# Attention and a gated two-layer network on one core: the largest of v spread by TensorE, stores issued by ScalarE from spare weight rows, five softmax buffers

## The chip, the cores and the metric

The kernel runs on one core of a Trainium2 chip. The metric is the device time of one execution in microseconds. The core has five engines that run their own instruction queues in order and meet at semaphores: TensorE (PE in the profile, with its weight loads as PEld), VectorE (DVE), ScalarE (ACT), GpSimd (POOL) and SyncE (SP), which here only issues DMAs.

## The reference, cut to what matters

Eight batches of eight heads, 576 queries and keys, 64 columns a head. Scores below the row's largest minus tau are dropped before the softmax. The result, 4608 tokens of 512 columns, goes through a network with 2048 hidden columns.

```python
scores = scale * np.matmul(q, k.transpose(0, 1, 3, 2))
thresh = np.max(scores, axis=-1, keepdims=True) - tau
scores = np.where(scores >= thresh, scores, -1000000000.0)
scores = scores - np.max(scores, axis=-1, keepdims=True)
attn = np.exp(scores)
attn = attn / (np.sum(attn, axis=-1, keepdims=True) + 1e-09)
x = np.matmul(attn, v)            # then heads side by side
h = x @ w_in
out = (h * (1.0 / (1.0 + np.exp(-h)))) @ w_out
```

Inputs of q, k, v are float32; the weights come as float64 and are decoded on the core.

## The kernel before

**Precision by halves.** Most products run on a high and a low half (hi + lo) of each factor: float16 for x, v, the attention weights, g and the layers' weights; the products hi·hi, hi·lo and lo·hi are summed in PSUM. To use float16's range, v and the weights are scaled by a power of two that comes from their largest magnitude.

**The scale of v.** For each batch, `vmax` (line 233) takes the largest magnitude of each of four loads of v per partition. `vscale` (line 243) calls `pow2_scales`, which reduces the four to one number per partition (`v_one`, line 110), spreads the largest over all partitions with GpSimd's `partition_all_reduce` (`v_all`, line 113), and works out the scale and its inverse with small VectorE instructions (`v_cl`, `v_e`, `v_sc`, lines 116 to 132). The scale is used where ScalarE and VectorE split v (lines 270 and 271) and in the factors of the network. The scales of the weights (`across=False`) don't go through line 113.

**Tiles of attention.** A tile is 128 queries of one head; there are 288, 36 in a batch. For a tile TensorE makes the scores in PSUM (line 406; line 394 for the first sixteen, which work in float32 throughout), VectorE their negative maximum (416) and threshold (419), ScalarE the exponential into a buffer `w32` (426), VectorE the mask and the sum (435) and the reciprocal (439, 443), ScalarE the division in place (448). GpSimd rounds the weights to float16 (459) and takes the low half (462 and 465) into `hl`; then `w32` is free again. SyncE issues DMA transposes of `hl` into `wT` (475), from which TensorE makes the product with v (490). There are four `w32` buffers and three of `hl`.

**Units of the network.** An h unit is twelve matmuls (524) into a PSUM bank, then tanh on ScalarE (532), a product on VectorE (533), the high half of g on ScalarE (541) and the low half on VectorE (547). An o unit is twelve matmuls (562) over a quarter of g; four quarters fill one bank, and after the fourth ScalarE copies it to a tile `o` of 128 x 288 (571) in one of two buffers and SyncE stores it (573): 64 stores in all. Both kinds and some others take their banks in turn from `bank` (two at first, three later).

**The order.** The loop at line 695 goes over tiles and calls the steps in slots; `todo` gives loads and splits of v, q and k their slots (a batch that starts at tile u has its `vscale` at u - 2, its first split of v at u + 4, its first product with v at u + 11), and `credit` spreads units among the tiles. The framework then orders each engine's queue by a simulated timeline and priorities, so steps can move ahead of their slots where their data and buffers allow. SyncE's one queue holds all loads, transposes and stores.

**The weights' tile.** `wst` (line 138) has 32 + 2 rows of 512 columns: raw weights are decoded two rows ahead of the split ones that take their place, so once all are split the last two rows hold nothing that is read again.

Of the kernel before, what the change touches and what calls it, by code (L numbers as in the profile page):

```python
# [10 lines left out]
BF16 = mybir.dt.bfloat16  # L11
# [8 lines left out]
P = 128  # L20
# [6 lines left out]
WID = 320  # L27
EXPMASK = 0x7F800000
GB = 17  # buffers of g: a group of 16 and one ahead
WSPARE = 2  # raw weights lie this far ahead of the split ones, which take their place  # L30
LOAD = 5  # tiles that the loads of q and k run ahead
AV_LAG = 3  # tiles from a visit's last to its product with v
EARLY = 36  # tiles in which ACT still rounds the weights of attention for GpSimd
GAP, GAP1 = 12, 1  # free slots before batch 0's second visits and before batch 1
V_SLOT = 26  # batch 0's values are split from here on
RATES = (1.3, 0.8)  # units of the experts per slot while batch 0's two groups are there
RATE = 0.95
# weights: first chunk, slots of the decoding and of the splitting, priority
W_PLAN = ((0, 0, 10, 13, 0), (16, 9, 22, 26, 150))
PRI_S, PRI_SOFT1, PRI_SOFT2 = 500, 50, 200  # L40

# a visit of two heads: its tiles of 128 queries (4: the last 64 of both heads) for the
# first and the second head, and the query ranges that it completes
VISITS = {
# [7 lines left out]
def attention_moe(  # L52
# [20 lines left out]

    # three banks in turn; the last one is for the sums of the weights while they come in
    turn = [0, 2]
# [5 lines left out]

    # ---------------------------------------------------------------- constants
    tau_sb = const.tile([P, 1], F32, name="tau_sb")
    nc.sync.dma_start(out=tau_sb, in_=tau)
    # 1/8 where the threshold can be met (tau >= 0), else 0: all scores equal, all kept
    gate = const.tile([P, 1], F32, name="gate")
# [7 lines left out]

    # stacks of (hi; lo) rows of q, with 64 zero columns for the shared tile
    qstack = []
# [8 lines left out]
    def pow2_scales(mx, name, across=True):  # L105
        """From mx [P, n] (bounds >= 0, per partition or, without across, the same on all):
        s = 2^(13-e) and 1/s for the largest's exponent e."""
        k = name[0]
        one = const.tile([P, 1], F32, name=f"{name}_one", tag=f"{k}_one")
        nc.vector.tensor_reduce(out=one, in_=mx, op=ALU.max, axis=AX.X)  # L110
        if across:
            allp = const.tile([P, 1], F32, name=f"{name}_all", tag=f"{k}_all")
            nc.gpsimd.partition_all_reduce(allp, one, P, bass.bass_isa.ReduceOp.max)
            one = allp
        cl = const.tile([P, 1], F32, name=f"{name}_cl", tag=f"{k}_cl")
        nc.vector.tensor_scalar(
            out=cl, in0=one, scalar1=2.0**-20, scalar2=2.0**47, op0=ALU.max, op1=ALU.min
        )
        e2 = const.tile([P, 2], I32, name=f"{name}_e2", tag=f"{k}_e2")
        nc.vector.tensor_scalar(  # L120
            out=e2[:, 0:1], in0=cl.bitcast(I32), scalar1=EXPMASK, scalar2=None, op0=ALU.bitwise_and
        )
        nc.vector.tensor_scalar(
            out=e2[:, 1:2], in0=cl.bitcast(I32), scalar1=EXPMASK, scalar2=EXPMASK,
            op0=ALU.bitwise_and, op1=ALU.bitwise_xor,
        )
        sc = const.tile([P, 2], F32, name=f"{name}_sc", tag=f"{k}_sc", bufs=3)
        nc.vector.tensor_scalar(
            out=sc[:, 0:1], in0=e2[:, 1:2].bitcast(F32), scalar1=2.0**12, scalar2=None, op0=ALU.mult
        )  # L130
        nc.vector.tensor_scalar(
            out=sc[:, 1:2], in0=e2[:, 0:1].bitcast(F32), scalar1=2.0**-13, scalar2=None, op0=ALU.mult
        )
        return sc

    # ---------------------------------------------------------------- weights
    NW = NK * 4 + NF
# [28 lines left out]
    def decode_weights(i):  # L166
        """float64 words to float32: the sign, 8 bits of the exponent (2^-112 on the top word
        read as float32 takes the exponent's bias down), 23 of the fraction."""
        t = wraw.pop(i)
# [13 lines left out]
        )  # L183
        # sums of the magnitudes over the rows of four chunks, four columns at a time: they
        # bound h (w_in), w_out
        n, c = divmod(i, 4)
# [31 lines left out]

    # ---------------------------------------------------------------- values
    vmx = {}  # L220
# [54 lines left out]

    # ---------------------------------------------------------------- q and k
    qkraw = {}
# [11 lines left out]
    def qcol(h, i):  # L289
        """Column of query tile i in the stack (even: 0..3, last, zeros; odd: zeros, last,  # L290
        2, 3, 0, 1)."""
        return i * P if h % 2 == 0 else (0, 384, 512, 128, 256)[(i + 1) % 5]
# [29 lines left out]

    # the first visits work in float32 throughout: the tensor engine has time for them
    direct = {}
# [51 lines left out]

    # ---------------------------------------------------------------- scores
    # a tile: (visit, [(head, query tile, first row, rows)])
    sps = {}
# [31 lines left out]
    def soft1(t):  # L411
        s_ps = sps[t]
        sm = sb.tile([P, 5], F32, tag="small", name=f"sm_{t}", bufs=4)
        w = sb.tile([P, S], F32, tag="w32", name=f"w32_{t}", bufs=4)
        negm, thr = sm[:, 0:1], sm[:, 1:2]
        nc.vector.tensor_reduce(  # L416
            out=negm, in_=s_ps[:, :, :HALF], op=ALU.max, axis=AX.XY, negate=True
        )
        nc.vector.tensor_scalar(
            out=thr, in0=negm, scalar1=-1.0, scalar2=ntau, op0=ALU.mult, op1=ALU.add  # L420
        )
        small[t] = sm
        wtile[t] = w
# [52 lines left out]

    # ---------------------------------------------------------------- attn @ v
    x16 = {}

    def av(v, p, c0, n):  # L480
        """w @ v of the pair's two heads, side by side in the columns of the array: (w hi + w lo) @
        v hi + w hi @ v lo."""
        b = visits[v][0]
# [29 lines left out]

    # ---------------------------------------------------------------- experts
    gt = {}
# [39 lines left out]
    def o_unit(b, c0, n, d, quarter):  # L555
# [11 lines left out]
        def post():  # L567
            if quarter < 3:
                return
            o = sb.tile([P, WID], F32, tag="o", name=f"ot_{b}_{c0}_{d}", bufs=2)  # L570
            nc.scalar.activation(o[:, :n], ps[:, :n], AF.Copy, scale=moe_sc[b][:, 1:2])
            c = b * S + c0
            nc.sync.dma_start(out=outT[d * P : (d + 1) * P, c : c + n], in_=o[:, :n])

# [8 lines left out]

    # ---------------------------------------------------------------- schedule
    visits = [(0, p, kind) for kind in ("low", "high") for p in range(NPAIR)]
# [195 lines left out]
```

## Time and profile before

| | us |
|---|---|
| median of three timed runs (lowest, highest) | 1358.73 (1357.87, 1359.26) |
| span of the profiled execution | 1360.4 |
| TensorE matmuls busy | 1183.7 (87%) |
| VectorE busy | 1002.8 (74%) |
| ScalarE busy | 817.5 (60%) |
| GpSimd busy | 789.9 (58%) |

The profile is one execution. "Busy" leaves out register, semaphore and DMA-issuing instructions. A slice line gives the busy share in tenths in 40 equal parts of the span. A line of waits reads: who waited, for whom, us in total, times, longest. A group's line reads: line, engine, operation, output and input, count, then busy us and mean ns of one, then idle time just before. A window's line gives start and end, length, busy us of PE, PEld, DVE, ACT and POOL (with counts), the TensorE clock that was granted as a share of full speed, the DMA share and GB/s. "Issue" as the end of an idle time means that nothing the profile shows was waited for.

### The profile page before, as it was taken

How to read it: one execution, taken by the hardware profiler on the slowest of the kernel's cores; microseconds unless marked ns; L12 is line 12 of the kernel's file. 1: busy time of each engine (PE TensorE's matmuls, PEld its weight loads, DVE VectorE, ACT ScalarE, POOL GpSimd, SP SyncE). 2: the span in 40 equal slices, each digit the busy share in tenths (PEclk: the TensorE clock that was granted, in tenths of full speed). 3: DMA queues.
4: the chain of work that ended last, by engine and by line, in shares of the span. 5: the costliest groups of instructions: out<-in, count | busy, mean ns of one | idle time of the engine just before them, and what ended most of it. 6: DMA issues, size and time to landing. Idle time of an engine off the chain costs nothing.

```text
span 1360.4 us, 26858 instructions
## 1 busy us (share of the span) xinstructions
PE 1183.7 (87%) x9392; PEld 899.9 (66%) x9392; DVE 1002.8 (74%) x2619; ACT 817.5 (60%) x1493; POOL 789.9 (58%) x964
## 2 busy tenths in 40 slices
PE   3774787898599979898899969899799999999998
PEld 2453555666477757676677757677577777777777
DVE  4987997897598967968497856869478787872421
ACT  3776775675476756656375745757367666662432
POOL 2647984787478656754476646556467666661000
PEclk9887888999799999999899979999799999999999
DMA  6454955778467656664475556565466565543000
GB/s 226 140 185 125 197 129 94 146 139 170 88 133 155 122 106 129 131 128 86 99 132 124 118 96 136 101 127 121 82 122 116 115 129 115 106 88 53 6 19 18
DMA packets 363479, 158.15 MB, mean 116 GB/s; under 512 B 329552, under 2 KB 338256, under 8 KB 363344
## 3 DMA queue, kind: packets, MB, share of 16 engines
q1 hardware_dynamic: 363344, 156.43, 55.5%
q8 instruction: 74, 1.21, 0.4%
q14 instruction: 61, 0.50, 0.1%
HBM read 66.72 MB, written 9.44 MB: 56 GB/s over the span
## 4 chain that ended last, share of the span: by engine, by line
DVE 35%; PE 34%; issue 13%; ACT 6%; POOL 6%; DMA 5%; SPq 2%; POOLq 0%; ACTq 0%; DVEq 0%
PE o L562 15%; PE h L524 8%; DVE w L435 8%; DVE sm L416 6%; DVE gbuf L547 6%; PE s L406 5%; PE a L490 5%; DVE qstack L310 3%; DVE th L533 3%; DMA vraw<-in_vL 2%; DMA wT<-hl 2%; ACT w L426 2%; POOL hl L459 2%; POOL hl L462 2%; ACT w L448 2%
## 5 line engine op out<-in xcount | busy, mean ns | idle before, releaser
L524 PE MATMUL h<-x,wst 128*128 128x288 f16 (+2 forms) x3072 | 422.3, 290 | 22.6 <-DVE th L533 19.1
L562 PE MATMUL o<-gbuf,wst 128*128 128x288 f16 (+2 forms) x3072 | 419.4, 293 | 22.4 <-DVE gbuf L547 16.1
L562 PEld LDWEIGHTS <-wst 128*128 128x128 f16 x3072 | 296.4, 100 | 117.1 <-issue 27.1
L459 POOL TENSOR_SCALAR hl<-w 128x576 f16<-128x576 f32 x264 | 187.3, 710 | 317.9 <-ACT w L448 69.1
L524 PEld LDWEIGHTS <-wst 128*128 128x128 f16 x3072 | 290.7, 99 | 119.2 <-issue 37.5
L462 POOL TENSOR_TENSOR hl<-w,hl 128x512 f16<-128x512 f32 x272 | 332.0, 1220 | 28.0 <-issue 13.9
L426 ACT ACTIVATE w<-s,sm 128x576 f32<-128x576 f32 x288 | 211.0, 736 | 204.5 <-POOL hl L465 135.4
L435 DVE SCALAR_TENSOR_TENSOR w<-s,sm,w 128x576 f32<-128x576 f32 x288 | 232.6, 810 | 110.4 <-ACT w L426 108.7
L448 ACT ACTIVATE w<-w,sm 128x576 f32<-128x576 f32 x288 | 218.2, 770 | 86.5 <-DVE sm L443 81.6
L416 DVE TENSOR_REDUCE sm<-s 128x1 f32<-128x576 f32 x288 | 215.1, 748 | 44.4 <-PE s L406 42.3
L406 PE MATMUL s<-khi,qstack 128*128 128x288 f32 x608 | 160.4, 346 | 70.0 <-DVE w L435 36.9
L547 DVE SCALAR_TENSOR_TENSOR gbuf<-th,gbuf 128x288 f16<-128x288 f32 (+2 forms) x256 | 167.3, 656 | 20.9 <-ACT gbuf L541 20.2
L406 PEld LDWEIGHTS s<-khi,qstack 128*128 128x128 f32 x608 | 98.5, 198 | 98.8 <-issue 71.4
L490 PE MATMUL a<-wT,v 128*64 128x288 f16 (+1 forms) x1680 | 142.4, 294 | 16.1 <-DMA wT<-hl 15.0
L532 ACT ACTIVATE th<-h,msc 128x288 f32<-128x288 f32 (+2 forms) x256 | 126.3, 495 | 49.5 <-DVE gbuf L547 30.0
L541 ACT ACTIVATE gbuf<-th 128x288 f16<-128x288 f32 (+2 forms) x252 | 109.9, 438 | 44.5 <-DVE th L533 43.9
L406 PE MATMUL s<-klo,qstack 128*128 128x288 f32 x608 | 134.2, 304 | 0.0
L533 DVE SCALAR_TENSOR_TENSOR th<-th,h 128x288 f32<-128x288 f32 (+2 forms) x256 | 113.2, 444 | 27.6 <-ACT th L532 25.4
L490 PEld LDWEIGHTS <-v 128*64 128x64 f16 x1680 | 91.3, 110 | 56.7 <-issue 41.9
L465 POOL TENSOR_TENSOR hl<-w,hl 128x64 f16<-128x64 f32 x272 | 115.3, 424 | 0.0
L406 PEld LDWEIGHTS s<-klo,qstack 128*128 128x128 f32 x608 | 102.2, 197 | 0.0
L320 POOL TENSOR_TENSOR klo<-kraw,khi 128x576 fp32r<-128x576 f32 x64 | 95.6, 1493 | 1.4 <-ACT khi L318 1.3
(82 smaller groups left out, 868.8 us busy)
## 6 DMA issues: line engine op xcount, KB each, us to landing
qraw<-in_qT SPq DMA_DIRECT2D x128, 144.0 KB, 3.0
kraw<-in_kT SPq DMA_DIRECT2D x128, 144.0 KB, 3.0
vraw<-in_vL SPq DMA_DIRECT2D x32, 320.0 KB, 3.5
wraw<-in_w_out SPq DMA_DIRECT2D x16, 512.0 KB, 4.0
out_t<-ot SPq DMA_DIRECT2D x56, 144.0 KB, 2.0
wT<-hl SPq DMA_TRANSPOSE x304, 3.3
gbuf<-in_w_in SPq DMA_DIRECT2D x8, 512.0 KB, 5.1
wraw<-in_w_in SPq DMA_DIRECT2D x8, 512.0 KB, 4.9
```

The costliest lines, as they stand in the source:

```text
L406: nc.tensor.matmul(s_ps[:, j, :HALF], lhs, kk[:, j * HALF : (j + 1) * HALF], start=(n == 0), stop=(n == len(seq) - 1),)
L416: nc.vector.tensor_reduce(out=negm, in_=s_ps[:, :, :HALF], op=ALU.max, axis=AX.XY, negate=True)
L426: nc.scalar.activation(wtile[t].rearrange("p (j c) -> p j c", j=2), sps[t][:, :, :HALF], AF.Exp, bias=small[t][:, 0:1],)
L435: nc.vector.scalar_tensor_tensor(out=w3, in0=s_ps[:, :, :HALF], scalar=sm[:, 1:2], in1=w3, op0=ALU.is_ge, op1=ALU.mult, accum_out=sm[:, 2:3],)
L448: nc.scalar.activation(w, w, AF.Copy, scale=r)
L459: nc.gpsimd.tensor_scalar(out=fl[:, 0:S], in0=w, scalar1=1.0, scalar2=1.0, op0=ALU.mult, op1=ALU.mult)
L462: nc.gpsimd.tensor_tensor(out=fl[:, 640:1152], in0=w[:, 0:512], in1=fl[:, 0:512], op=ALU.subtract)
L490: nc.tensor.matmul(a_ps[odd * D : (odd + 1) * D, :n], vt[:, lo_v, odd, kv, :], wT[v, b * H + 2 * p + odd][:, kw, c0 - base : c0 - base + n ...
L524: nc.tensor.matmul(ph[:, :n], wi(c, f, lo_w), x16[b, lo_x][:, c, c0 : c0 + n], start=(k == 0), stop=(k == 11),)
L533: nc.vector.scalar_tensor_tensor(out=th[:, :n], in0=th[:, :n], scalar=1.0, in1=ph[:, :n], op0=ALU.add, op1=ALU.mult,)
L547: nc.vector.scalar_tensor_tensor(out=g[:, 1, :n], in0=th[:, :n], scalar=2.0**-14, in1=g[:, 0, :n], op0=ALU.mult, op1=ALU.subtract,)
L562: nc.tensor.matmul(ps[:, :n], wo(f, d, lo_w), g[:, lo_g, :n], start=(f == 0 and k == 0), stop=(f == NF - 1 and k == 2),)
```

## The change

Four edits. In `pow2_scales`, ScalarE multiplies the identity by `v_one`, so that each partition's largest stands on the diagonal of a 128 x 128 bfloat16 tile; TensorE multiplies this with a matrix of ones into a PSUM bank, which puts all 128 values on every partition; VectorE takes their maximum. In `soft1`, `w32` has five buffers. In `o_unit`, the copy goes to one of the two spare rows of `wst`, and the store is issued on ScalarE's queue. (Comments are removed too, so line numbers shift by 5 or 6 behind line 115.)

```diff
         if across:
-            allp = const.tile([P, 1], F32, name=f"{name}_all", tag=f"{k}_all")
-            nc.gpsimd.partition_all_reduce(allp, one, P, bass.bass_isa.ReduceOp.max)
-            one = allp
+            diag = const.tile([P, P], BF16, name=f"{name}_diag", tag="diag")
+            nc.scalar.activation(diag, ident, AF.Copy, scale=one)
+            allp = bank([P, P], f"{name}_ps")
+            nc.tensor.matmul(allp, ones, diag, start=True, stop=True)
+            one = const.tile([P, 1], F32, name=f"{name}_all", tag=f"{k}_all")
+            nc.vector.tensor_reduce(out=one, in_=allp, op=ALU.max, axis=AX.X)
...
-        w = sb.tile([P, S], F32, tag="w32", name=f"w32_{t}", bufs=4)
+        w = sb.tile([P, S], F32, tag="w32", name=f"w32_{t}", bufs=5)
...
-            o = sb.tile([P, WID], F32, tag="o", name=f"ot_{b}_{c0}_{d}", bufs=2)
+            o = wst[:, NW + d % 2, :]
             nc.scalar.activation(o[:, :n], ps[:, :n], AF.Copy, scale=moe_sc[b][:, 1:2])
             c = b * S + c0
-            nc.sync.dma_start(out=outT[d * P : (d + 1) * P, c : c + n], in_=o[:, :n])
+            nc.scalar.dma_start(out=outT[d * P : (d + 1) * P, c : c + n], in_=o[:, :n])
```

The change moves instructions on every engine. Three places follow. A number in a name counts the program's buffers and differs between the two programs; `w_229` is the softmax buffer of tile 229, and the brackets name the semaphores that an instruction waits for (DMAHW0 to 7 are those of DMAs).

GpSimd's queue at tiles 229 to 231 before: the two `ISA` rows without names at lines 113 and 459 stand around the reduction and set GpSimd up for what comes next.

```order
L465 TENSOR_TENSOR hl_12029<-w_229_11976,hl_12029 128x64
L459 TENSOR_SCALAR hl_12081<-w_230_12019 128x576 [waits DMAHW7_49,Activation_49]
L113 ISA
L113 ISA v_all<-v_one 128x1 [waits DVE_49]
L459 ISA
L459 TENSOR_SCALAR hl_12163<-w_231_12071 128x576 [waits DMAHW0_49,Activation_49]
L462 TENSOR_TENSOR hl_12081<-w_230_12019,hl_12081 128x512 [waits Pool_49]
L465 TENSOR_TENSOR hl_12081<-w_230_12019,hl_12081 128x64
```

GpSimd's queue at the same tiles with the change:

```order
L470 TENSOR_TENSOR hl_12020<-w_229_11967,hl_12020 128x64
L464 TENSOR_SCALAR hl_12071<-w_230_12010 128x576 [waits DMAHW5_49,DVE_49]
L464 TENSOR_SCALAR hl_12153<-w_231_12061 128x576 [waits DMAHW7_49,Activation_49]
L467 TENSOR_TENSOR hl_12071<-w_230_12010,hl_12071 128x512 [waits Pool_49]
L470 TENSOR_TENSOR hl_12071<-w_230_12010,hl_12071 128x64
L467 TENSOR_TENSOR hl_12153<-w_231_12061,hl_12153 128x512 [waits Pool_49]
```

The reduction and both set-up rows are gone from between the roundings of the weights.

VectorE's queue where it takes up the spread maximum, near tile 232, before (`v_one` and `v_cl` are those of batch 7, which starts at tile 265; `gbuf` is g, `sm` the small numbers of a tile):

```order
L110 TENSOR_REDUCE v_one<-vmx_12088 128x1 [waits DVE_49]
L547 SCALAR_TENSOR_TENSOR gbuf<-th_288_14_11815,gbuf 128x288 [waits Activation_49]
L533 SCALAR_TENSOR_TENSOR th_288_15_11853<-th_288_15_11853,h_288_15_11802 128x288 [waits Activation_49]
L439 TENSOR_SCALAR sm_12148<-sm_12148 128x1 [waits DVE_49]
L443 RECIPROCAL sm_12148<-sm_12148 128x1 [waits DVE_49]
L416 TENSOR_REDUCE sm_12230<-s_12152 128x1 [waits PE_49]
L116 TENSOR_SCALAR v_cl<-v_all 128x1 [waits Pool_49]
L310 SCALAR_TENSOR_TENSOR qstack_85<-qraw_50_12246,gate,qstack_85 64x576 [waits DMAHW4_49,Activation_49]
```

VectorE's queue at the same place with the change (`v_ps` is TensorE's product; these are the numbers of batch 6, which starts at tile 229):

```order
L552 SCALAR_TENSOR_TENSOR gbuf<-th_288_15_11841,gbuf 128x288 [waits Activation_49]
L448 RECIPROCAL sm_12219<-sm_12219 128x1 [waits DVE_49]
L421 TENSOR_REDUCE sm_12247<-s_12223 128x1 [waits PE_49]
L119 TENSOR_REDUCE v_all<-v_ps 128x1 [waits PE_49]
L424 TENSOR_SCALAR sm_12247<-sm_12247,ntau 128x1 [waits DVE_49]
L121 TENSOR_SCALAR v_cl<-v_all 128x1 [waits DVE_49]
L125 TENSOR_SCALAR v_e_11889<-v_cl 128x1 [waits DVE_49]
```

The wait for GpSimd has become one for TensorE, and the scale of a batch now comes about 36 tiles later: before, it ran a batch ahead; now it stands where the batch begins.

ScalarE's queue around a store, near tile 240, before (`ot` is the copied tile, `v_6_3` the split of v):

```order
L448 ACTIVATE w_239_12530<-w_239_12530,sm_12529 128x576 [waits DVE_49]
L571 ACTIVATE ot_288_2_12212<-o_288_2_12054,msc_9812 128x288 [waits DMAHW7_49,PE_49]
L508 ACTIVATE x_5_0_10605<-a_3_288_12183 128x288 [waits PE_49]
L270 ACTIVATE v_6_3_13828<-vraw_3_11235,v_sc 128x640
L426 ACTIVATE w_240_12572<-s_12533,sm_12571 128x576 [waits Activation_49,Pool_49]
```

ScalarE's queue at the same place with the change:

```order
L453 ACTIVATE w_239_12518<-w_239_12518,sm_12517 128x576 [waits DVE_49]
L577 ACTIVATE wst<-o_288_2_12045,msc_9808 128x288 [waits DMAHW6_49,PE_49]
L453 ACTIVATE w_240_12560<-w_240_12560,sm_12559 128x576 [waits DVE_49]
L579 DMA out_t<-wst 128x288 [waits DMAHW0_49,Activation_49]
L323 ACTIVATE khi_12879<-kraw_52_12757 128x576 [waits PE_49]
L314 ACTIVATE qstack_85<-qraw_52_12756,gate 128x576 [waits DMAHW2_49,PE_49]
```

The store now stands in ScalarE's queue, here one instruction behind its copy; it waits for that copy and for a semaphore of an earlier DMA.

## The prediction

> **What bounds the kernel now.** I read the page's busy shares and slices first, to see which engine is full and where it isn't.
>
> ```profile
> PE 1183.7 (87%) x9392; PEld 899.9 (66%) x9392; DVE 1002.8 (74%) x2619; ACT 817.5 (60%) x1493; POOL 789.9 (58%) x964
> ...
> PE   3774787898599979898899969899799999999998
> ...
> DVE 35%; PE 34%; issue 13%; ACT 6%; POOL 6%; DMA 5%; SPq 2%; POOLq 0%; ACTq 0%; DVEq 0%
> ```
>
> TensorE (PE) is nearly full from the eighth slice on, except in a few dips that come at about equal distances. The third line is the chain that ended last: 13% of the span is "issue", time that waits for nothing the profile shows. Next, the instructions of line 113 on GpSimd (POOL), and of the list of waits (us in total, times, longest) what GpSimd and ScalarE (ACT) wait for.
>
> ```profile
> L113 POOL PARTITION_ALL_REDUCE v_all<-v_one x8: 377/378/379, 19.1 to 957.3; - x8
> ...
> POOL v_all L113 <- issue: 43.9, 7, 7.5
> ACT w L426 <- POOL hl L465: 135.4, 54, 14.4
> ```
>
> Each of the eight reductions takes 0.38 us, yet GpSimd idles ahead of seven of them for 43.9 us with nothing to wait for. The timeline at the last one (start, us, engine, line; in brackets the idle time before and what ended it) shows that it idles behind them too, and what that does to the others.
>
> ```profile
> 957.33 0.38 POOL L113 PARTITION_ALL_REDUCE v_all<-v_one  x1 [5.91 <-issue]
> ...
> 957.74 0.15 DVE L116 TENSOR_SCALAR v_cl<-v_all 128x1 f32<-128x1 f32 x1 [5.84 <-POOL v_all L113]
> ...
> 959.53 3.28 PE L562 MATMUL o<-gbuf,wst 128*128 128x288 f16 x13 [4.97 <-DVE gbuf L547]
> ...
> 964.73 0.67 POOL L459 TENSOR_SCALAR hl<-w 128x576 f16<-128x576 f32 x1 [7.03 <-issue]
> ...
> 966.83 0.74 ACT L426 ACTIVATE w<-s,sm 128x576 f32<-128x576 f32 x1 [13.41 <-POOL hl L465]
> ```
>
> GpSimd loses 5.91 + 7.03 us round a 0.38 us instruction. VectorE (DVE) stands at line 116 for 5.84 us, with the rounding of g behind it, so TensorE runs dry for 4.97 us; and ScalarE waits 13.41 us for a softmax buffer that GpSimd still holds. The windows give this by stage (busy us of PE, PEld, DVE, ACT, POOL; then the granted clock):
>
> ```profile
> 90.00:125.00 35.00, 19.95 (x108) 13.97 (x109) 26.15 (x66) 22.48 (x43) 17.91 (x18) 0.74 0.43 126
> 125.00:210.00 85.00, 63.35 (x437) 45.23 (x436) 84.28 (x183) 62.78 (x111) 75.95 (x79) 0.84 0.73 161
> 210.00:240.00 30.00, 24.86 (x179) 19.23 (x178) 18.19 (x56) 15.15 (x24) 14.65 (x22) 0.84 0.49 86
> ...
> 330.00:390.00 60.00, 39.48 (x287) 30.31 (x287) 42.42 (x118) 32.63 (x57) 34.89 (x44) 0.83 0.58 114
> 390.00:480.00 90.00, 84.57 (x715) 65.35 (x712) 82.76 (x214) 65.29 (x121) 68.23 (x84) 1.00 0.73 140
> 480.00:510.00 30.00, 23.93 (x180) 17.95 (x179) 18.32 (x57) 14.99 (x25) 16.65 (x24) 0.94 0.48 100
> ...
> 635.00:670.00 35.00, 25.55 (x181) 19.29 (x179) 18.04 (x59) 15.82 (x26) 18.21 (x24) 0.85 0.40 83
> ...
> 790.00:825.00 35.00, 23.90 (x178) 18.25 (x178) 18.26 (x57) 14.98 (x25) 17.28 (x23) 0.80 0.42 78
> 825.00:945.00 120.00, 111.80 (x945) 86.08 (x944) 95.57 (x250) 76.68 (x143) 70.40 (x89) 1.00 0.61 121
> 945.00:990.00 45.00, 35.73 (x266) 26.70 (x264) 23.98 (x73) 19.87 (x34) 21.56 (x29) 0.85 0.46 91
> 990.00:1240.00 250.00, 246.75 (x2084) 191.03 (x2081) 197.73 (x527) 163.49 (x306) 164.80 (x207) 1.00 0.60 112
> ```
>
> Six of these (210, 330, 480, 635, 790, 945) hold a reduction each. In them all engines idle together and the clock is 0.80 to 0.94; in those between (390, 825) TensorE is busy 196.37 of 210 us, 93.5%, at clock 1.00. After 990 there is no reduction, and it is busy 98.7%. So TensorE bounds the kernel, and the reductions are holes in it.
>
> **Part 1: the reduction leaves GpSimd.** What it removes, for the six later holes, I work out in three ways. The chain of waits holds their "issue" pieces directly (start, us, what; the two early holes, then the first and the last piece of the six later ones, and two rows for the clock):
>
> ```profile
> 12.53 6.55 issue
> ...
> 100.80 7.29 issue
> ...
> 216.67 1.31 issue
> ...
> 957.78 6.96 issue
> ...
> 969.87 5.96 PE o L562 x32
> ...
> 1333.10 23.53 PE o L562 x192
> ```
>
> From 216.67 us to 957.78 us there are twelve such pieces at the six reductions, 50.5 us in sum. By the windows without the clock: the six last 235 us, TensorE works 173.45 us in them; at 93.5% that takes 185.5 us, so 49.5 us are lost. With the clock: 173.45 us weighted by each window's clock is 147.4 us of full-speed work, 157.6 us at 93.5%, a loss of 77.4 us; that counts slow clock as loss even where TensorE was not the last to finish. The chain tells how much of it lies on the path: 32 matmuls take 5.96 us behind the last hole and 32/192 of 23.53, 3.92 us, in the tail: 2 us a hole, 12 us for six. I take 50.5 + 12 = 62, of 49 to 77. The Trainium skill's page "TensorE: Matmul & The Clock Gate", Part 1, holds that an idle window of about 3.4 us halves the clock until a busy one has passed; an estimate by that page is 1.7 us a hole, 10 us in place of 12, and the windows' clocks agree in kind.
>
> The two early holes stand in the chain with 6.55 and 7.29 us. There VectorE is the limit: 84.28 of 85 us after 125, but 26.15 of 35 us in the window with the hole, 8.6 us short. I take 12 for both, of 0 (the loads and decoding are late next) to 15. Together 74 us. Late next is TensorE: in the stretches between the holes the next fullest engine, VectorE, is busy 82.76 of 90 us at most, so it, GpSimd and ScalarE can carry the faster pace.
>
> What it adds, eight times: a 128x128 activation, a weight load and a 128x128 matmul, a reduction from PSUM. The trace has all of these shapes but the weight load, which overlaps matmuls (count, then busy us and mean ns of one; the last row is a wait):
>
> ```profile
> L362 ACT ACTIVATE wT<-tl 128x128 f32<-128x128 f32 x16 | 4.4, 277 | 0.0
> L191 PE MATMUL wps<-wst,ones 128*128 128x128 bf16 x128 | 13.9, 244 | 10.8 <-DVE wst L180 10.5 <-DVE sm L439 0.3
> L196 DVE TENSOR_REDUCE wmx<-wps 128x1 f32<-128x128 f32 x8 | 2.2, 280 | 0.1
> DVE sm L416 <- PE s L406: 42.3, 43, 2.7
> ```
>
> TensorE's own share is 8 x 0.244 = 2.0 us, all on the path: 2. ScalarE and VectorE get 2.2 us each, hidden behind TensorE. New is a wait: in the order VectorE stands at the reduction of the product until TensorE has come to it, with softmax and the rounding of g queued behind. Its nearest row is the softmax maximum's wait for scores, 1 us in the mean and 2.7 at most: 0 to 22 us for eight. TensorE is working in that time, so I take 4. The scale is also ready later: tied to a PSUM bank it now comes in its place, a batch later in the order, just ahead of ScalarE's splitting of v (slot 4 of a batch); the first product with v stands at slot 11, and those seven tiles cover it. Part 1 is worth 74 - 6 = 68 us.
>
> **Part 2: stores issued by ScalarE.**
>
> ```profile
> L573 SPq DMA_DIRECT2D out_t<-ot x64: 332/508/1622, 230.8 to 1357.2; - x64
> SPq L573 <- ACT ot L571: 47.0, 15, 6.7
> PE a L490 <- DMA wT<-hl: 15.0, 5, 8.8
> ```
>
> Sixty-four issues at 508 ns are 32.5 us that go from SyncE's queue to ScalarE, which is 60% busy; behind a store on ScalarE stand exponentials and tanh. If ScalarE's 6% of the chain holds for them, 2 us reach the path. Bounds: all 64 at 1622 ns passed on whole, 104 us lost; or a gain, since SyncE stood 47.0 us between 240 and 1230 us (the second row) waiting for a store's data with transposes behind it: TensorE waited for transposes 15.0 us in all, 8.8 of that in one hole, so at most 15. I take a loss of 2, nearest to the median issue. The page "DMA: Bandwidth & Descriptors" of the Trainium skill (Issuing engines are not separate DMA queues) speaks against this part: DMAs from any engine interleave on the same 16 DMA engines, and spreading them only saves issue time. By that rule the part brings nothing; with nothing in place of my loss of 2, the time would be 1291 us. The spare rows give two buffers, as before, so no store waits longer for its buffer; the last store still follows the last ScalarE copy.
>
> **Part 3: the fifth softmax buffer.** The 135.4 us that ScalarE waits for GpSimd to free a buffer is the wait that this could shorten. But 13.41 us stood at one hole; eight such are 107 us, and they go with part 1. From 990 on the same wait is there without any hole:
>
> ```profile
> ACT w L426 <- POOL hl L465: 26.4, 15, 4.6
> ```
>
> TensorE is 98.7% busy all the same. So I take 0, of 0 to 5 us gained (the bound is the longest of these waits).
>
> **The sum.** 68 - 2 + 0 = 66 us. The profiled execution's span is 1360.4 us, so 1294.4; the median of the timed runs is 1358.7, 1.7 under that span, which gives 1292.7, or 1293 us.
>
> **Rivals.**
> Everything comes back (the larger gain). All clock loss is on the path and SyncE, freed of the stores, feeds transposes earlier: 77 + 15 + 5 + two thirds of the 15, less the costs of 2, gives up to 105 us, 1254 us. For it: all engines idle together in the holes. Against: the chain holds 12 us of slow clock, not 27.
>
> The wait moves. VectorE stands at the product for TensorE, and ScalarE at the splitting of v for the scale, in the same places as the old holes: 50 + 7 us gained, 22 lost to the one and as much again to the other at worst; with half of the second 24 us in all, 1335 us. For it: both queues are in order, and the scale has lost its batch of lead. Against: TensorE has work through these waits, as it had not in the holes.
>
> Slower, by the stores. Each of the 64 holds ScalarE for its issue, for the end of its own copy and for a DMA semaphore last used by a transfer on SyncE's queue, which may be late; th and g behind it are late, and TensorE runs out. It decides from 68 / 64 = 1.1 us a store reaching TensorE; at the longest issue, 1.62 us, the time is 1358.7 - 68 + 104 = 1395 us. Against: after 990 ScalarE waited for buffers fifteen times, 1.8 us in the mean, and TensorE stayed at 98.7%, so TensorE has more than that in hand.
>
> Nothing happens: GpSimd's idle time belongs to its own switch between kinds of work and stays, or its place is taken at once by the next late engine. 1359 us. Against: the pieces stand only at line 113, and the new order has no such instruction.
>
> **How the numbers follow.** Forecast (gain 50 to 82 us): 0.56. Larger gain: 0.20. The wait moves: 0.15. Slower by the stores: 0.05. Nothing: 0.04. The range, 1256 to 1328 us, takes in the forecast, nearly all of the larger gain, whose end is 1254, and two thirds of the moved wait. A measurement of this kernel tells 0.2%, 2.7 us, from no change: so faster 0.92 (the first three, and 0.01 of the last), same 0.03, slower 0.05.
>
> **What would show it.** Right: no line-113 reduction and no POOL "issue" pieces beside it; TensorE over 93% busy at clock 0.95 or more in every window from 240 us on; a v_all wait on VectorE under 2.7 us each; the ScalarE wait for buffers down from 135.4 us to under 40. Wrong: dips of TensorE at the same seven places with VectorE's v_all or ScalarE's split of v as what ended them; or th and g waiting behind store issues, with TensorE's wait for g over 40 us.

## The result, and the profile after

| | before | after |
|---|---|---|
| median of the timed runs, us (lowest, highest) | 1358.99 (1357.87, 1360.19) | 1295.8 (1293.03, 1299.93) |
| ratio, 95% interval | | 0.9528 (0.9504 to 0.9552) |
| span of the profiled execution, us | 1360.4 | 1294.1 |
| mean granted TensorE clock | 0.950 | 0.967 |

63 us are gone; 66 were forecast. Ratios, here and below, are taken over fast runs alone: of the runs below, one of 2926.22 us (part 3 alone) stands in its median, but not in its ratio. The page of after, busy shares, TensorE's slices and clock, and the chain by engine:

```profile
PE 1179.7 (91%) x9400; PEld 894.8 (69%) x9400; DVE 1014.3 (78%) x2627; ACT 825.0 (64%) x1501; POOL 791.1 (61%) x956
...
PE   5676789798899989998999989999999999999998
...
PEclk8987889899999989999999999999999999999999
...
PE 35%; DVE 34%; DMA 9%; issue 8%; ACT 7%; POOL 6%; SPq 0%; ACTq 0%; POOLq 0%; DVEq 0%
```

From the ninth slice on none is under 8, where four of before were (5, 7, 6, 7); "issue" has gone from 13% to 8% of a shorter chain; and GpSimd has eight instructions fewer. TensorE's busy time, though, has fallen by only 4.0 us. The new instructions, grouped by shape (count, then busy us and mean ns, then idle time before them):

```profile
L115 ACT ACTIVATE v_diag<-ident,v_one 128x128 bf16<-128x128 f32 x8 | 3.2, 396 | 4.8 <-DVE v_one L110 4.8
L119 DVE TENSOR_REDUCE v_all<-v_ps 128x1 f32<-128x128 f32 x8 | 2.2, 278 | 0.0
L117 PE MATMUL v_ps<-v_diag,ones 128*128 128x128 bf16 x8 | 1.8, 219 | 0.0
```

VectorE never idles ahead of line 119: the product is ready each time it gets there. The rows of the list of waits that the prediction named or that are new:

```profile
POOL klo L325 <- ACT khi L323: 97.6, 15, 12.2
...
DVE w L440 <- ACT w L431: 92.2, 87, 7.2
ACT w L431 <- POOL hl L470: 70.3, 31, 6.3
...
PE s L411 <- DVE w L440: 43.9, 36, 6.4
...
DVE vmx L238 <- DMA vraw<-in_vL: 18.9, 13, 3.4
```

ScalarE's wait for softmax buffers has halved (135.4 before), and its longest piece has gone from 14.4 to 6.3 us. The first row is new in size: GpSimd, on its way to the low half of k (`klo`, line 325), waits 97.6 us for ScalarE's high half (`khi`). No row of TensorE waiting for g (line 552) is left. What is left of the dips, by windows (start, end, length, busy us of PE, PEld, DVE, ACT, POOL, clock):

```profile
306.00:340.00 34.00, 26.76 (x202) 21.05 (x200) 30.02 (x85) 24.08 (x41) 28.23 (x36) 0.90 0.80 148
442.00:476.00 34.00, 28.94 (x218) 22.30 (x216) 25.98 (x73) 20.03 (x34) 22.21 (x27) 0.90 0.60 130
...
748.00:782.00 34.00, 29.57 (x239) 22.21 (x237) 22.93 (x58) 16.20 (x27) 18.86 (x24) 0.95 0.61 125
...
986.00:1240.00 254.00, 251.68 (x2114) 193.74 (x2113) 158.85 (x412) 138.00 (x263) 117.71 (x149) 1.00 0.44 83
```

The places are those where v is split and the next v is loaded, and TensorE is busy 79 to 87% in them, 99% after them. The timeline at the third shows what it waits for there:

```profile
748.80 1.65 DVE L276 SCALAR_TENSOR_TENSOR v<-vraw,v_sc,v 128x640 f16<-128x640 f32 x1
...
752.02 1.05 SPq L232 DMA_DIRECT2D vraw<-in_vL  x2
...
755.21 0.82 DVE L238 TENSOR_REDUCE vmx<-vraw 128x1 f32<-128x640 f32 x1 [2.96 <-DMA vraw<-in_vL]
...
756.90 0.50 PE L411 MATMUL s<-khi,qstack 128*128 128x288 f32 x2 [2.63 <-DVE w L440]
```

VectorE, in its order, stands 2.96 us at the largest of v until a load that SyncE issued at 752.02 has landed; the mask of the softmax (line 440), which frees the scores' bank, comes behind it, and TensorE stands for it. That is a wait of another kind than the one removed, in the same places. In the second window the same pair of waits stands (3.0 us at the load, 4.6 us for the mask). The first differs: VectorE is busy 30.02 of its 34 us, and TensorE's longest waits there, 2.6 and 1.8 us, end with small VectorE instructions (the network's factors, line 266, and a threshold, line 424), not with the mask.

### The profile page after: what moved, and what is told of

It is laid out like the page before. It is cut to its first block, busy times and chain, and to the rows that moved or that the text cites. A ratio compares the mean times of both kernels' runs of the same rounds, so it can differ in the third digit from the quotient of the medians.

```text
span 1294.1 us, 26850 instructions
## 1 busy us (share of the span) xinstructions
PE 1179.7 (91%) x9400; PEld 894.8 (69%) x9400; DVE 1014.3 (78%) x2627; ACT 825.0 (64%) x1501; POOL 791.1 (61%) x956
## 4 chain that ended last, share of the span: by engine, by line
PE 35%; DVE 34%; DMA 9%; issue 8%; ACT 7%; POOL 6%; SPq 0%; ACTq 0%; POOLq 0%; DVEq 0%
PE o L567 15%; PE h L529 9%; DVE w L440 8%; DVE sm L421 6%; PE s L411 6%; DVE gbuf L552 5%; DMA wT<-hl 5%; PE a L495 4%; DVE qstack L315 4%; DVE th L538 3%; DMA vraw<-in_vL 3%; ACT w L431 3%; POOL hl L467 2%; POOL hl L464 2%; ACT w L453 2%
## 5 line engine op out<-in xcount | busy, mean ns | idle before, releaser
L567 PE MATMUL o<-gbuf,wst 128*128 128x288 f16 (+2 forms) x3072 | 407.6, 289 | 5.5 <-DVE wst L211 2.6
L431 ACT ACTIVATE w<-s,sm 128x576 f32<-128x576 f32 x288 | 211.3, 737 | 174.3 <-POOL hl L470 70.3
L440 DVE SCALAR_TENSOR_TENSOR w<-s,sm,w 128x576 f32<-128x576 f32 x288 | 232.7, 812 | 94.9 <-ACT w L431 92.2
L411 PE MATMUL s<-khi,qstack 128*128 128x288 f32 x608 | 159.8, 345 | 53.0 <-DVE w L440 43.9
L552 DVE SCALAR_TENSOR_TENSOR gbuf<-th,gbuf 128x288 f16<-128x288 f32 (+2 forms) x256 | 171.4, 673 | 25.1 <-ACT gbuf L546 24.5
L325 POOL TENSOR_TENSOR klo<-kraw,khi 128x576 fp32r<-128x576 f32 x64 | 95.8, 1497 | 119.6 <-ACT khi L323 97.6
L495 PE MATMUL a<-wT,v 128*64 128x288 f16 (+1 forms) x1680 | 147.5, 294 | 4.8 <-DMA wT<-hl 2.7
L470 POOL TENSOR_TENSOR hl<-w,hl 128x64 f16<-128x64 f32 x272 | 117.9, 433 | 0.0
```

Source lines behind the costliest of these rows:

```text
L411: nc.tensor.matmul(s_ps[:, j, :HALF], lhs, kk[:, j * HALF : (j + 1) * HALF], start=(n == 0), stop=(n == len(seq) - 1),)
L431: nc.scalar.activation(wtile[t].rearrange("p (j c) -> p j c", j=2), sps[t][:, :, :HALF], AF.Exp, bias=small[t][:, 0:1],)
L440: nc.vector.scalar_tensor_tensor(out=w3, in0=s_ps[:, :, :HALF], scalar=sm[:, 1:2], in1=w3, op0=ALU.is_ge, op1=ALU.mult, accum_out=sm[:, 2:3],)
L495: nc.tensor.matmul(a_ps[odd * D : (odd + 1) * D, :n], vt[:, lo_v, odd, kv, :], wT[v, b * H + 2 * p + odd][:, kw, c0 - base : c0 - base + n ...
L552: nc.vector.scalar_tensor_tensor(out=g[:, 1, :n], in0=th[:, :n], scalar=2.0**-14, in1=g[:, 0, :n], op0=ALU.mult, op1=ALU.subtract,)
L567: nc.tensor.matmul(ps[:, :n], wo(f, d, lo_w), g[:, lo_g, :n], start=(f == 0 and k == 0), stop=(f == NF - 1 and k == 2),)
```

## The experiments

The spread by TensorE is called part 1 here, the stores part 2, the fifth buffer part 3.

**Part 1 alone.** The kernel before with only this of the change:

```diff
-            nc.gpsimd.partition_all_reduce(allp, one, P, bass.bass_isa.ReduceOp.max)
...
+            nc.scalar.activation(diag, ident, AF.Copy, scale=one)
...
+            nc.tensor.matmul(allp, ones, diag, start=True, stop=True)
...
+            nc.vector.tensor_reduce(out=one, in_=allp, op=ALU.max, axis=AX.X)
```

> The kernel before with only the spread of the largest moved to TensorE; stores, their buffers and the four softmax buffers as before. Theory (the reduction's holes on GpSimd are the whole gain): 1290 to 1303 us, ratio 0.95 to 0.96. Rival (stores leaving SyncE, or the fifth buffer, bring a good part): 1315 us or more.

1282.65 us (1280.71 to 1288.51), ratio 0.9411 (0.935 to 0.9471): faster than the whole change. Its busy times and four of its waits:

```profile
PE 1164.7 (91%) x9400; PEld 893.0 (70%) x9400; DVE 1003.9 (78%) x2627; ACT 819.3 (64%) x1501; POOL 794.8 (62%) x956
```

```profile
DVE w L438 <- ACT w L429: 61.9, 56, 5.3
...
PE s L409 <- DVE w L438: 27.8, 23, 4.1
...
POOL klo L323 <- ACT khi L321: 9.6, 6, 3.0
...
PE a L493 <- DMA wT<-hl: 7.4, 6, 2.0
```

With the same 9400 matmuls TensorE is busy 15.0 us less than in after, and the wait at `klo` is a tenth. So the first part carries all of the gain, and the other two together take some of it away. The 1290 to 1303 us that were expected are missed: it is faster.

**Part 2 alone.** The stores on ScalarE's queue from the spare rows, in the kernel before:

```diff
-            o = sb.tile([P, WID], F32, tag="o", name=f"ot_{b}_{c0}_{d}", bufs=2)
+            o = wst[:, NW + d % 2, :]
...
-            nc.sync.dma_start(out=outT[d * P : (d + 1) * P, c : c + n], in_=o[:, :n])
+            nc.scalar.dma_start(out=outT[d * P : (d + 1) * P, c : c + n], in_=o[:, :n])
```

> The kernel before with only the stores changed: copies into the spare weight rows, stores issued by ScalarE. Theory: nothing to a small loss, 1356 to 1366 us. Rival (SyncE's freed queue feeds transposes earlier): 1335 us or less. Rival (ScalarE held by issues): 1375 us or more.

1350.64 us (1343.94 to 1355.68), ratio 0.9911 (0.9879 to 0.9942): 8 to 16 us gained where the holes still are, and between the 1335 us of the one rival and the 1356 us that were expected at the least. It isn't the transposes' wait that went. TensorE's wait for them, 15.0 us in 5 before, is here:

```profile
PE a L490 <- DMA wT<-hl: 16.8, 6, 8.8
```

The gain lies between the reductions: from the fifth of them to the last it is 467.3 us in before (490.0 to 957.3) and 454.8 here (489.1 to 943.9), and from there to the end 403.1 and 402.4. What gave it isn't taken apart; with the edit TensorE's order of matmuls, too, differs at 661 of 9392 places.

**Part 3 alone.** Five buffers and the spare rows, stores still on SyncE:

```diff
-        w = sb.tile([P, S], F32, tag="w32", name=f"w32_{t}", bufs=4)
+        w = sb.tile([P, S], F32, tag="w32", name=f"w32_{t}", bufs=5)
...
-            o = sb.tile([P, WID], F32, tag="o", name=f"ot_{b}_{c0}_{d}", bufs=2)
+            o = wst[:, NW + d % 2, :]
```

> The kernel before with five softmax buffers; the copies go to the spare weight rows to make room, the stores stay on SyncE. Theory: 1350 to 1360 us, as the buffers cover one tile of some three that a hole costs. Rival (a fifth buffer lets ScalarE run through the holes): 1335 us or less.

1355.53 us median, ratio 0.9966 (0.9932 to 1.0001): none or a little gained. Its waits:

```profile
ACT w L426 <- POOL hl L465: 98.7, 43, 8.0
POOL klo L320 <- ACT khi L318: 94.2, 16, 12.9
...
POOL v_all L113 <- issue: 45.0, 7, 7.9
```

The fifth buffer does shorten ScalarE's wait, from 135.4 to 98.7 us, and brings the wait at `klo` with it. Neither shows in the time; I take it that the reductions' holes, 45.0 us ahead of line 113, set it, which no run shows.

**A reduction on GpSimd that nobody reads.** To tell the holding of GpSimd from VectorE's wait for the result, after with one GpSimd reduction per batch added:

```diff
+            junk = const.tile([P, 1], F32, name=f"{name}_junk", tag="junk")
+            nc.gpsimd.partition_all_reduce(junk, one, P, bass.bass_isa.ReduceOp.max)
```

> The changed kernel, plus GpSimd's reduction of each batch put back beside the new way, with a result that nobody reads: GpSimd has its holes again, VectorE doesn't wait for them. Theory (GpSimd's own idle time is what costs, through the softmax buffers): most of the gain goes, 1335 to 1360 us. Rival (VectorE's wait at v_cl with its queue behind it was the path): 1296 to 1312 us. In between the two share it.

1328.97 us (1327.44 to 1331.99), ratio 0.9743 (0.9695 to 0.9792): 33 of the 63 us come back, between the two ranges that were expected. But for the added rows, the engines execute the same instructions in the same order as in after, so the 33 us don't come from another order. The timeline at the last of them:

```profile
947.41 0.38 POOL L115 PARTITION_ALL_REDUCE v_junk<-v_one  x1 [6.77 <-DVE x L516]
955.13 1.39 POOL L327 TENSOR_TENSOR klo<-kraw,khi 128x576 fp32r<-128x576 f32 x1 [7.34 <-issue]
...
958.72 0.74 ACT L433 ACTIVATE w<-s,sm 128x576 f32<-128x576 f32 x1 [5.40 <-POOL hl L472]
```

GpSimd still stands 6.77 + 7.34 us round 0.38 us, and ScalarE 5.40 us for a softmax buffer; that alone costs 33 us, 4.1 a reduction. The rest of what part 1 gains is put down to the waits for the result, VectorE's at line 116 among them: 30 us of the 63, or 46 of the 79 that part 1 is worth beside four buffers (below). That is a difference; no run takes it apart. GpSimd's idle time was not the whole cause.

**Two of them, one behind the other.** Is it the instruction that holds GpSimd, or the change of kind? After with the unread reduction followed by another:

```diff
+            nc.gpsimd.partition_all_reduce(junk, one, P, bass.bass_isa.ReduceOp.max)
+            junk2 = const.tile([P, 1], F32, name=f"{name}_junk2", tag="junk2")
+            nc.gpsimd.partition_all_reduce(junk2, junk, P, bass.bass_isa.ReduceOp.max)
```

> The changed kernel with two of GpSimd's reductions a batch put back, one right behind the other, results unread. One of them gave 1328.97 us. Theory (the idle time belongs to the switch to this kind of instruction and back, not to the instruction): 1326 to 1336 us, the second one 0.4 us behind the first. Rival (each reduction brings its own idle time): 1350 us or more.

1338.34 us (1333.73 to 1345.75), ratio 0.9856 (0.9806 to 0.9906). That is 9 us more than with one by the medians, 15 by the ratios and 5.0 by the spans of the two traces (1331.9), over the 1326 to 1336 us of the theory and under the 1350 of the rival. The last pair, and the rows of lines 115 and 117 for GpSimd's change of kind, `MODIFY_POOL_CONFIG` (count, ns, first and last start):

```profile
951.40 0.38 POOL L115 PARTITION_ALL_REDUCE v_junk<-v_one  x1 [6.14 <-DVE w L444]
951.88 0.35 POOL L117 PARTITION_ALL_REDUCE v_junk<-v_junk  x1
959.09 1.40 POOL L329 TENSOR_TENSOR klo<-kraw,khi 128x576 fp32r<-128x576 f32 x1 [6.86 <-issue]
...
L115 POOLq MODIFY_POOL_CONFIG  x16: 3/6/19, 12.0 to 945.5; - x16
L117 POOL PARTITION_ALL_REDUCE v_junk<-v_junk x8: 350/350/352, 20.5 to 951.9; - x8
```

The second follows within 0.1 us and takes 0.35, and line 117 has no such row of its own. The idle time lies on either side of the pair, not of each (5.8 to 8.0 us ahead of the eight pairs, 6.7 to 7.2 behind them): it belongs to GpSimd's going over to this kind of instruction and back. The trace names that step: two `MODIFY_POOL_CONFIG` rows stand ahead of each reduction or pair and two right behind it. There are 34 such rows in the trace of before, as in those of both of these kernels, and in after only the two that stand at the kernel's start. Those ahead of the reductions in before:

```profile
L113 POOLq MODIFY_POOL_CONFIG  x16: 4/9/13, 11.6 to 951.7; - x16
```

Why the second costs 5 to 15 us of the time, more than its own 8 x 0.45 us, stays open: the order is after's here too, and the four times of this kernel lie 12 us apart. (What the profile names as the releaser ahead of the first differs from place to place, line 444 of VectorE here and "issue" at others; behind the pair it is "issue".)

**Which of the two other parts takes the gain away.** After with the stores on SyncE, and after with four buffers:

```diff
-            nc.scalar.dma_start(out=outT[d * P : (d + 1) * P, c : c + n], in_=o[:, :n])
+            nc.sync.dma_start(out=outT[d * P : (d + 1) * P, c : c + n], in_=o[:, :n])
```

> The changed kernel with its stores back on SyncE (still from the spare weight rows); five softmax buffers stay. The reduction alone gave 1282.65 us, the whole change 1295.8, so some 13 us went to the other two parts. Theory (the fifth buffer costs them, by the order that the queues get from it): 1290 to 1304 us, GpSimd's wait for the split of k on ScalarE at 80 us or more. Rival (the stores on ScalarE cost them): 1277 to 1288 us.

```diff
-        w = sb.tile([P, S], F32, tag="w32", name=f"w32_{t}", bufs=5)
+        w = sb.tile([P, S], F32, tag="w32", name=f"w32_{t}", bufs=4)
```

> The changed kernel with four softmax buffers; stores stay on ScalarE. Theory (the fifth buffer costs the 13 us): 1270 to 1287 us, GpSimd's wait for the split of k under 30 us. Rival (the stores on ScalarE cost them): 1290 to 1304 us.

With SyncE's stores and five buffers 1295.2 us, ratio 0.9517 (0.948 to 0.9555), no better than the whole change, though TensorE's order differs from it at 2062 of 9400 places. With ScalarE's stores and four buffers 1285.81 us, ratio 0.9453 (0.942 to 0.9485). What waits for `khi` in the first and in the second, from the views of `klo`'s line:

```profile
  ACT khi L323: 112.6, 18
```

```profile
  ACT khi L323: 6.3, 5
```

So it is the fifth buffer, and the wait at `klo` comes and goes with it, whoever issues the stores. Where the time goes: windows from 716 to 956 us, where both are within 5 us of the same tile (the 181st softmax maximum starts at 720.2 and 715.6 us), of after and then with four buffers:

```profile
716.00:956.00 240.00, 228.62 (x1869) 172.73 (x1868) 196.43 (x524) 158.53 (x290) 147.48 (x182) 0.99 0.61 119
```

```profile
716.00:956.00 240.00, 227.68 (x1920) 177.29 (x1920) 201.01 (x538) 161.07 (x298) 162.14 (x196) 1.00 0.63 127
```

TensorE is "busy" alike, at a like clock, but does 51 matmuls less in after, and GpSimd 14 instructions less. A page of the Trainium skill, "Perfetto Trace Analysis" (Identifying the Most-Contended Engine), warns that matmul busy time says little, since matmuls are pipelined, and has one look at the share of the weight loads. The traces agree: the matmuls' share of the span is 91% in after and with four buffers alike, and the weight loads, 172.73 against 177.29 us here, tell the two apart.

**The scale earlier.** For the dips that are left: part 1 alone with `vscale` five slots earlier, so that its chain is done before the batch begins.

```diff
-        at(u - 2 if b else 1, lambda b=b: vscale(b))
+        at(u - 7 if b else 1, lambda b=b: vscale(b))
```

> The reduction alone on TensorE, as in the run of 1282.65 us, with the scale of v five slots earlier. Theory (the dips left at the starts of batches come from the late scale, which keeps v's buffers and so the next loads of v late): 1270 to 1280 us. Rival (they come from something else at a batch's start): 1280 to 1288 us.

1306.84 us (1305.72 to 1309.18), ratio 0.9609 (0.9578 to 0.964): 24 us slower than part 1 alone. The theory that the late scale makes the dips, 1270 to 1280 us, is not borne out, though an effect of the new order may hide one of the scale. Who waits for the reduction of the product, and TensorE's wait for transposes, here:

```profile
  PE h L527: 9.0, 4
```

```profile
PE a L493 <- DMA wT<-hl: 20.8, 10, 6.7
```

A unit of the network now waits for the product's PSUM bank, and TensorE waits longer for transposes than in part 1 alone (7.4 us). That is 9 + 13 of the 24 us; that these two rows are the cause is argued, not shown.

**The splitting of k earlier.** To take the wait at `klo` away with five buffers, and the same edit with four as its control:

```diff
-            at(use - 3, lambda h=h: split_k(h))
+            at(use - 4, lambda h=h: split_k(h))
```

> The whole change, with the splitting of k (on which GpSimd's klo follows ScalarE's khi) put one slot earlier in the order, at four slots ahead of its use instead of three. Open is why the fifth buffer costs about 10 us where it stands beside the new reduction. Theory: with five buffers GpSimd reaches klo before ScalarE has written khi and stands there in its order (97.6 us in 15 waits, against 6.3 us in 5 with four buffers); asked for earlier, khi is there in time: the wait falls below 40 us and the time comes to 1280 to 1290 us. Rival: that wait costs nothing in itself, since GpSimd has spare time, and the 10 us come from how the work of all engines falls together: 1291 to 1302 us, whatever becomes of the wait.

> The control for the run before: the same earlier splitting of k in the kernel that has the TensorE spread alone (four buffers, stores on SyncE), whose klo hardly waits (9.6 us in 6). Theory and rival agree that there is nothing to win: 1278 to 1290 us, as without it. Outside of that, a shift of one slot by itself moves the time by more than the fifth buffer does, and a difference of 10 us between two orders is not a sign of any one wait.

1290.69 us (1288.31 to 1296.75), ratio 0.9497 (0.9461 to 0.9533), and 1284.12 us (1281.79 to 1285.42), ratio 0.944 (0.9408 to 0.9472). The first lies between the theory's 1280 to 1290 us and the rival's 1291 to 1302, and it tells nothing between the two, for its wait at `klo` is the old one to the digit:

```profile
POOL klo L325 <- ACT khi L323: 97.6, 15, 11.3
```

The edit didn't do what it was for: the framework put each splitting back where it had been, and no engine executes an instruction at another place than in the kernel it was made from. What these two runs are good for is scatter, with the next two, of the same instructions in the same order.

**Both again on that chip.** Part 1 alone and the whole change, unchanged:

> The spread by TensorE alone, a second time and on another chip beside the whole change. If the first part carries all of the gain and the other two together cost about 1%, 1278 to 1288 us, a ratio of 0.938 to 0.948, and at least 7 us under the whole change in this job. If the first result belonged to its noisy chip: 1290 us or more.

> The whole change again, beside the three others on one chip: 1292 to 1300 us, a ratio of 0.950 to 0.956.

Part 1 alone: 1279.34 us (1275.73 to 1285.91), ratio 0.9404 (0.9373 to 0.9436). The whole change: 1293.82 us (1289.69 to 1297.71), ratio 0.9513 (0.9477 to 0.9549). Part 1 alone is 14.5 us faster on one chip, and its slowest run is under the fastest of the whole change. The pairs of like order differ by 4.8 us (1279.34 and 1284.12) and 3.1 us (1290.69 and 1293.82), so less than about 5 us isn't read from these runs.

## Why the prediction was right, and where it was not

The number came out, 1293 against 1295.8, but with luck: two of its terms were off by about as much in opposite directions. Gains from the ratios times 1359 us; part 1 alone is the mean of the three runs in its order, the two controls among them (80, 76 and 81), and so is the whole change (64, 68 and 66):

| term | forecast | measured |
|---|---|---|
| part 1 | 68 | 79 |
| part 2, beside part 1 | -2 | 0 (five buffers: 66 against 66) to -5 (four: 74 against 79) |
| part 3, beside part 1 | 0 (0 to 5 gained) | -8 (66 against 74) to -13 (66 against 79) |
| sum | 66 | 66 |

The -5 and the -13 hold the move of the copies to the spare rows too; the -8 is the fifth buffer's alone.

**The early holes: 12, measured about 13.** The last decoding of a weight stands behind both, so its start shows them; these are rows of before and of after (ns of one, then first and last start in us):

```profile
L180 DVE SCALAR_TENSOR_TENSOR wst<-wraw,wst x24: 666/693/1639, 40.3 to 175.7; 128x512 int32<-128x512 int32 x24
```

```profile
L185 DVE SCALAR_TENSOR_TENSOR wst<-wraw,wst x24: 666/1037/1758, 23.6 to 161.4; 128x512 int32<-128x512 int32 x24
```

It starts 14.3 us earlier, and with part 1 alone 12.5 (163.2). VectorE was the limit there, as the prediction had it.

**The later holes: undersized.** Part 1 alone has a span 79.6 us shorter, 67 of it behind the decoding; after the costs the prediction gave 62 - 6 = 56. Of the missing 11 us, 4 are the wait at the product, which isn't there (the 0.0 of line 119, where the bounds were 0 to 22): VectorE comes to it when TensorE has long done it. The clock may give another 4: I had 2 us a hole, 12 for six, and behind the decoding TensorE's busy time fell by 18.9 us in part 1 alone (1074.36 to 1055.44), some 3 of them for 28 matmuls that come earlier, as the clock there rose from 0.96 to 0.99. That all of it is the clock's is not shown. By the page "TensorE: Matmul & The Clock Gate" of the Trainium skill (Part 1) I had estimated 1.7 a hole, 10 for six; on this reading the trace lies above both. What is left, about 3 us, is within the scatter. TensorE's own 8 x 219 ns (1.8 of 2 us) were right; the activation took 396 ns, not 277, hidden as expected.

**The stores: right.** At 338 ns an issue on ScalarE, of 64, no wait of TensorE for g came, and putting them back on SyncE changed nothing with five buffers. That agrees with the rule of the Trainium skill ("DMA: Bandwidth & Descriptors", Issuing engines are not separate DMA queues) that spreading them saves issue time alone. Alone they gained 8 to 16 us, which the prediction allowed (up to 15) but for a reason, TensorE's wait for transposes, that its trace doesn't show.

**The fifth buffer: the step that failed.** "So I take 0, of 0 to 5 us gained" reasoned from the wait that the buffer shortens, and that it would only help or be idle. It did shorten that wait. What the step left out is that a framework which orders queues by its own simulated timeline gives another order for another count of buffers. In GpSimd's queue the `klo` of seven heads in a row, from the 32nd on, stand at rows

```
five buffers: 456  459  487  488  514  517  543
four buffers: 458  472  487  501  514  532  543
```

With four they come about 14 rows apart; with five every second stands next to the one before, some 13 rows too early, while ScalarE's `khi` for it stays 17 to 26 rows behind the one before in ScalarE's queue (rows 727, 753, 778, 795 and 819 for the last five of the seven, store issues counted). GpSimd then stands there, 6.5 us in the mean (97.6 / 15), with the roundings of the weights behind it; VectorE waits more for exponentials (92.2 us, 61.9 in part 1 alone) and TensorE more for the mask (43.9, 27.8). That the buffer costs 8 us, or 13 with the spare rows, is shown. That it does so by this wait fits every kernel beside part 1, but is not shown: the edit meant to remove the wait left it; part 3 alone has 94.2 us of it and loses nothing; and TensorE's idle time as a whole is no longer in after (1294.1 - 1179.7 = 114 us) than in part 1 alone (1280.8 - 1164.7 = 116), so the loss lies within what counts as busy. The other kernels say the same: TensorE is busy 1173.7 to 1179.7 us in the four traces with part 1, five buffers and no reduction on GpSimd, and 1162.6 to 1167.6 in the four with part 1, four buffers and the scale in its place (1172.0 with the scale earlier).

TensorE's own queue accounts for a part of it. The product with v, in matmuls of 128 x 64, comes in stretches between the others. There are 164 to 168 such stretches in every kernel with four buffers and 185 to 191 in every kernel with five; in part 1 alone 164, in after 191. In after a matmul starts 61 ns behind the one before it inside a stretch and 129 ns outside, but 218 ns where a stretch begins and 227 where it ends (means over the starts that lie under 0.3 us apart). One more stretch thus costs about 218 + 227 - 61 - 129 = 255 ns, and 27 more are 7 us, all of it time that counts as busy. That is an estimate from the traces, and no run changes the stretches alone; but part 3 alone, with 24 more than before (189 against 165), has TensorE busy 5.9 us longer, and 24 x 0.255 is 6.1. By this estimate TensorE's own order makes 7 of the 8 to 13 us; what the rest is stays open.

**What would show it.** No reduction at line 113: right. The v_all wait under 2.7 us: right, 0. TensorE's wait for g under 40: right, none. Buffers under 40: wrong, 70.3 with five and 74.8 in part 1 alone with four; I had read nearly the whole wait into the holes, and half of it was not theirs. TensorE over 93% at clock 0.95 in every window: wrong, 79 to 87% at 0.90 to 0.95 in the windows above; in two of the three the load of v has taken over, which was neither of the two new waits of the rival.

**The rivals.** The larger gain (up to 105 us) put 27 us of slow clock on the path, the forecast 12; the 16 us by which TensorE's busy time fell above (18.9 - 3) lie between, and SyncE gave nothing. The moved wait came neither at the product nor at the splitting of v; its like came at the load, and small. Slower by the stores: from 1.1 us a store; measured at most 5 / 64 = 0.08. Nothing happens: its reason, that GpSimd's idle time belongs to its own switch, proved true, and its conclusion false, since the switch went with the instruction. What I set against it, that the "issue" pieces stand only at line 113, holds for GpSimd and not for the chain: 64 of the chain's 173 us of "issue" in before (12.7%) stand at the eight reductions, and after still has 8%.

## What to carry to other kernels

A short instruction can hold its engine for much longer than it takes: look at the idle time on both sides of it, and at who stands behind it on the other queues. Time the parts of a change one by one and beside each other: here the smallest kernel, with the TensorE spread alone, is the fastest (1279 to 1284 us), and a right sum hid a part that costs 8 to 13 us. Where a framework orders the queues, one more buffer is a new order on every engine, so read the order, not the wait that the buffer was for. And a change that leaves the order as it was, like the reduction that nobody reads, tells more than one that changes it.

## What the runs showed of the hardware

- GpSimd's reduction over partitions takes 0.38 us, but 5.8 to 7.5 us of idle GpSimd ahead of it and 6.7 to 7.4 behind it (before); a second one directly behind it takes 0.35 us and brings no idle time of its own. The trace has a `MODIFY_POOL_CONFIG` pair at each end.
- Eight such reductions with their results unread made the kernel 33 us longer, 4.1 each; with the results waited for they were worth about 10 each (79 / 8, beside four buffers).
- TensorE's busy time isn't a measure of its work: 1179.7 and 1164.7 us for the same 9400 matmuls. The clock differs (0.967 and 0.973), but from 716 to 956 us, at like clocks, 1869 matmuls in after and 1920 with four buffers filled like busy times.
- A change between matmuls of 128 x 128 and of 128 x 64 costs time on TensorE: starts lie 218 and 227 ns apart at the two ends of a stretch in after, 129 and 61 ns outside and inside.
- A store was issued in 338 ns on ScalarE's queue, 508 ns in the median on SyncE's.
